# A Strassen MLP on one NeuronCore: another order of the two-level first-layer products, their sums on VectorE in quarters, residual rows added beside the fifth product, weight-sum copies issued by SyncE

## The chip, the core and the metric

The kernel runs on one core of a Trainium2 chip. Five engines with a queue each work side by side: TensorE (PE: matmul, and PEld for the weight loads), VectorE (DVE), ScalarE (ACT), GpSimd (POOL) and SyncE (SP, which here only issues DMAs). The metric is the device time of one execution in microseconds, as the median of several runs; less is better. The profile is of one further execution.

## The reference

Everything is fp32. A linear attention with a decay per head is followed by a Fourier mixing, a layer norm and an MLP; what the change touches is the MLP.

```python
x = attention(q, k, v, lam)                    # (4, 8, 768, 64) -> (4, 768, 512)
u = x + np.real(np.fft.fft(np.fft.fft(x, axis=1), axis=2))
un = (u - mean(u)) / np.sqrt(var(u) + 1e-06)   # over the 512 columns
ch = np.maximum(un @ w_ch1, 0.0) @ w_ch2       # w_ch1 (512, 2048), w_ch2 (2048, 512)
return u + ch                                  # (4, 768, 512)
```

## The kernel before

The 3072 rows go through the MLP as twelve groups of 256 rows. Four groups (PLAIN) pass a plain MLP (`mlp`, lines 636 and 650) while attention and mixing still run. The other eight (LATE) are taken as four pairs of groups, j = 0 to 3, after about 430 us, and this is the part that the change touches. Of a pair, the two layers of the MLP are computed as 2x2 block products by a Strassen scheme (Winograd's form): seven products of sums of blocks instead of eight products of blocks. `PRODUCTS` names the seven: a is a sum of weight blocks (first layer) or of hidden blocks (second layer), b the other operand.

The first layer of pairs 0 and 1 (`first_layer`, matmuls on L882) has one level. The second layer of all pairs (`deep_second`, L1023) and the first layer of pairs 2 and 3 (`deep_first`, L964) have two levels: each of the seven products is itself made of seven partial products (`seven`). A partial product is eight weight loads and eight matmul records of 128x128, into one of three PSUM banks X, Y, Z of the product: X takes partial products 0, 2, 4 and 6, Y takes 1, Z takes 3 and 5, and each must have been read before the next is put on it. The read (`read`, L971/L973 in the first layer, L1029/L1031 in the second) adds the bank to a quarter of a hidden tile; the first value of a fresh tile is copied by ScalarE instead, four of a product's seven.

The hidden tiles of a pair are `a11`, `a12`, `a22`, `s1` (also called T) and `s3` (a21). In `deep_first` products 0 to 6 come in order and are gathered into these: after product 1, T is added to a11 (L986, GpSimd) and a11 gets its relu; after product 3, a12 = T + a22 (L989, GpSimd); after product 4, a21 += T on GpSimd (L991), a22 += a21 on VectorE (L992), relu of a22, the loads of the residual rows (`load_x`), the splits (`split`, L847: one quarter becomes the difference of two) and the preparation of the second layer's first operand (`prepare_a`, L861 to L865). The helper `part_sum` does a sum in two halves of 128x1024, all on its line L939.

The sums of the second operands (`inputs`, L796 to L815 on VectorE, then nine 128x128 sums on GpSimd, L820 to L822) are made before the pair's first layer. The second-level sums of the weights are made once on GpSimd during the first layers of pairs 0 and 1 (`keep_sums`, `keep_sums_w`), put to HBM, and loaded as tiles `tx` product by product (L760, SyncE; six buffers, so two products). One of the four weight sums of a product is copied into the place of a quarter of the weights by `place_sums_w` (L745, seven DMAs issued by ScalarE).

In `deep_second` the outputs are gathered into y11, y12, y21, y22 and a tile T (`P.t`): after product 3, y21 = T + y22 (L1054, VectorE) and the residual rows are added on GpSimd (`add_u`, L1037); after product 4, y12 += T and y22 += y12 (L1057, L1058, VectorE), the residual of y22 on GpSimd (L1037) and that of y12 on VectorE (L1060, rows read backwards). Then rows are stored, one half by an indirect DMA of GpSimd (L625), the other by SyncE (L623).

The order is set by `in_step`: product k begins at step 7k and takes every second step, so that two products alternate on TensorE; the preparations of product k + 1 go between. The tile framework's scheduler then orders each engine's queue and sets semaphores; a queue is worked off in order.

```python
X, Y, Z = (bank() for _ in range(3))
for m, ps, start, where in ((0, X, True, (0, 0, 1)), (1, Y, True, (0, 0, 0)), (2, X, False, (1, 0, 1)), ...
    mm(m, ps, start)
    read(ps, *where)
    yield 0.0
```

Of the kernel before, what the change touches and what calls it, by code (L numbers as in the profile page):

```python
# [76 lines left out]
def kernel(  # L77
# [10 lines left out]
    nc = tc.nc  # L88
# [639 lines left out]
    def quarters_w(t):  # L728

        return [t[:, k, f:f + FH // 2] for f in (0, FH // 2) for k in range(2)]  # L730
# [11 lines left out]
    def place_sums_w():  # L742

        for k, (a, _) in enumerate(PRODUCTS):
            nc.scalar.dma_start(quarters_w(s2.A[a])[2], s2.sd[k][3])  # L745

# [26 lines left out]
    def inputs(j):  # L773
# [40 lines left out]
        yield 0.0  # L814
        V.tensor_tensor(t4, b21, t2, op=SUB)  # L815
        yield 0.0
        q2, q1, q4 = [new(s2.hp, [128, 3, 128], "sv", bufs=3) for _ in range(3)]
        for i, n in enumerate(("t2", "t1", "t4")):
            C11, C12, C21, C22 = (U[n][:, k, m:m + 128] for k in range(2) for m in (0, 128))
            nc.gpsimd.tensor_tensor(q2[:, i], C12, C11, op=ADD)  # L820
            nc.gpsimd.tensor_tensor(q1[:, i], C22, q2[:, i], op=SUB)
            nc.gpsimd.tensor_tensor(q4[:, i], C21, q2[:, i], op=SUB)  # L822
            P.T[n] = [q1[:, i], q2[:, i], q4[:, i]]
            yield 0.0
# [115 lines left out]

    def seven(mm, read, first=()):

        X, Y, Z = (bank() for _ in range(3))
        for m, ps, start, where in ((0, X, True, (0, 0, 1)), (1, Y, True, (0, 0, 0)), (2, X, False, (1, 0, 1)),
                                    (3, Z, True, (1, 1, 1)), (4, X, False, (1, 1, 0)), (5, Z, False, (1, 0, 0)),
                                    (6, X, False, (0, 1, 1))):
            mm(m, ps, start)
            read(ps, *where)
            yield 0.0

    def deep_first(j, k):

        P = pairs[j]
        h, (a, b) = P.h, PRODUCTS[k]
        y, fresh = (("s1", 1), ("a11", 1), ("a22", 1), ("s1", 0), ("s3", 1), ("a12", 0), ("s3", 0))[k]
        A11, A12, A3, A22 = quarters_w(s2.A[a])
        B11, T3, B21, B22 = (P.U[b][:, kt, m:m + 128] for kt in range(2) for m in (0, 128))
        (S1, S2, S4), (T1, T2, T4) = P.pre_w.pop(k), P.T[b]
        ab = [(A11, B11), (A12, B21), (S2, T2), (A3, T3), (S1, T1), (A22, T4), (S4, B22)]
# [7 lines left out]
        def read(ps, r, s, first):  # L967
# [6 lines left out]
            done[r, s] = done.get((r, s), 0) + 1  # L974
            if k > 4 and done[r, s] == (1 if (r, s) == (0, 1) else 2):
                nc.scalar.activation(o, o, AF.Relu)

        yield from seven(mm, read)

        def relu(t):  # L980
            for s in range(G):
                nc.scalar.activation(t[:, s], t[:, s], AF.Relu)

        T, a11, a12, a21, a22 = (h[n] for n in ("s1", "a11", "a12", "s3", "a22"))
        if k == 1:
            part_sum(nc.gpsimd, a11, a11, T, ADD)  # L986
            relu(a11)
        elif k == 3:
            part_sum(nc.gpsimd, a12, T, a22, ADD)  # L989
        elif k == 4:  # L990
            part_sum(nc.gpsimd, a21, a21, T, ADD)  # L991
            part_sum(V, a22, a22, a21, ADD)  # L992
            relu(a22)
            load_x(j)
            open_y(j)
            split(a11)
            run(prepare_a(j, 0))
        elif k == 5:
            split(a22)
            split(a12)  # L1000
        elif k == 6:
            split(a21)
            part_sum(V, T, a21, a22, ADD)
            if j + 1 < PAIRS:
                load_u(j + 1)

    def deep_second(j, k):
# [26 lines left out]

        def add_u(k, m, y):
            u = P.us[k][:, :, 0:HM] if m == 0 else P.us[k][:, :, DM - 1:HM - 1:-1]
            nc.gpsimd.tensor_tensor(y, y, u, op=ADD)  # L1037

        who, yt = P.who, P.yt
        if k == 0:  # L1040
            h["s2"] = h["a11"]
            if j < DEEP:
                split(h["s1"])
            part_sum(V, h["a11"], h["s1"], h["a11"], SUB)
        elif k == 1:
            V.tensor_tensor(y11, y11, T, op=ADD)  # L1046
            add_u(0, 0, y11)
        elif k == 2:
# [4 lines left out]
        elif k == 3:  # L1053
            V.tensor_tensor(y21, T, y22, op=ADD)  # L1054
            add_u(1, 0, y21)
        elif k == 4:
            V.tensor_tensor(y12, y12, T, op=ADD)  # L1057
            V.tensor_tensor(y22, y22, y12, op=ADD)  # L1058
            add_u(1, 1, y22)
            V.tensor_tensor(y12, y12, P.us[0][:, :, DM - 1:HM - 1:-1], op=ADD)  # L1060
        elif k == 5:
# [26 lines left out]
    def deep_pair(j):  # L1088

        def before(k):  # L1090
            if k == 0:
                return both(prepare_w(j, 0), inputs(j))
            return prepare_w(j, k)

# [13 lines left out]
    def in_step(work):  # L1108
# [3 lines left out]
        for at in range(7 * n + 8):  # L1112
# [5 lines left out]
            for q in sorted(live, key=abs):  # L1118
                if q < 0 or (at - 7 * q) % 2 == 0:
                    if next(live[q], live) is live:  # L1120
                        del live[q]

    def late():
        for j in range(PAIRS):
            if j < DEEP:
# [4 lines left out]
                if j + 1 < DEEP:  # L1130
                    in_step(second_layer(j) + [(inputs(j + 1), iter(()))])
        place_sums_w()
        in_step(second_layer(DEEP - 1) + [w for j in range(DEEP, PAIRS) for w in deep_pair(j)])
# [115 lines left out]
```

## Time and profile before

| | |
|---|---|
| time, median of 3 runs | 817.17 us (815.62 to 818.04) |
| the profiled execution's own time | 810.14 us |
| its span | 808.4 us |
| granted TensorE clock | 0.997 of full speed |
| busy: TensorE, VectorE, ScalarE, GpSimd | 95%, 72%, 27%, 27% of the span |
| chain that ended last, by engine | TensorE 71%, VectorE 13%, DMA 7%, issue 4% |

By stretch, the part that the change touches (us busy; the columns are the stretch, TensorE, VectorE, ScalarE, GpSimd):

| stretch | what runs | PE | DVE | ACT | POOL |
|---|---|---|---|---|---|
| 430 to 475 | pair 0, first layer | 44.8 | 42.7 | 10.9 | 38.5 |
| 475 to 520 | pair 0, second | 44.6 | 35.3 | 5.0 | 5.1 |
| 520 to 560 | pair 1, first | 40.0 | 32.9 | 9.4 | 35.3 |
| 560 to 613 | pair 1, second | 51.0 | 42.2 | 6.9 | 8.6 |
| 613 to 667 | pair 2, first (two levels) | 51.0 | 33.3 | 17.4 | 19.6 |
| 667 to 711 | pair 2, second | 43.5 | 37.9 | 5.5 | 8.2 |
| 711 to 760 | pair 3, first (two levels) | 46.0 | 30.7 | 16.7 | 16.4 |
| 760 to 801 | pair 3, second | 40.5 | 31.9 | 4.8 | 5.2 |

A line of the profile names the source line, the engine, the operation, the output and input tiles without their numbers, and the shape; in a timeline the first two columns are the start from the span's beginning and the duration in us, and in brackets stands how long the engine stood idle before it and what ended that. In a table of waits an entry reads "who waited <- for whom", with the total in us, how often, and the longest. A matmul in fp32 shows as two weight loads and two matmul records.

### The profile page before, as it was taken

What the parts mean: (1) busy time and instruction counts of PE and PEld (TensorE: products, weight loads), DVE (VectorE), ACT (ScalarE), POOL (GpSimd) and SP (SyncE); (2) the same over time, 40 slices, a digit from 0 to 9 for tenths busy, and PEclk for the clock granted to TensorE, in tenths of its full rate; (3) what the DMA queues carried; (4) which work ended last, traced back from release to release, by engine and by line L of the source; (5) the groups of instructions that cost most, each with busy time, mean ns of one, the idle gap of its engine ahead of it and who ended that gap; (6) DMA issues with size and microseconds to landing.
All of it is one profiled execution on the core that took longest, in us unless ns stands there. A gap on an engine that the chain in (4) does not pass through costs nothing.

```text
span 808.4 us, 14556 instructions
## 1 busy us (share of the span) xinstructions
PE 770.1 (95%) x5616; PEld 642.5 (79%) x5616; DVE 580.9 (72%) x1126; ACT 215.5 (27%) x504; POOL 216.3 (27%) x202
## 2 busy tenths in 40 slices
PE   6889899999999999999999999999999989999896
PEld 5777666768585857767747899988899989999896
DVE  6899898775744571345897997689866489836983
ACT  3655444225420210312101221022101331032400
POOL 3233340011020110220106930298013330235011
PEclk9999999999999999999999999999999999999998
DMA  9979624248831137440333384256845446455442
GB/s 239 249 156 256 194 81 132 66 104 208 213 100 58 53 70 152 118 162 28 65 69 125 133 272 125 76 206 230 291 125 166 136 149 191 132 162 162 125 118 79
DMA packets 152331, 116.80 MB, mean 144 GB/s; under 512 B 113998, under 2 KB 113998, under 8 KB 152262
## 3 DMA queue, kind: packets, MB, share of 16 engines
q1 hardware_dynamic: 146112, 101.56, 45.3%
q10 hardware_dynamic: 4038, 7.61, 2.6%
q0 software_dynamic: 2112, 6.69, 2.5%
q8 instruction: 45, 0.74, 0.4%
q14 instruction: 24, 0.20, 0.1%
HBM read 83.58 MB, written 32.25 MB: 143 GB/s over the span
## 4 chain that ended last, share of the span: by engine, by line
PE 71%; DVE 13%; DMA 7%; issue 4%; ACT 2%; POOL 2%; POOLq 0%; ACTq 0%; SPq 0%; DVEq 0%
PE p L1023 19%; PE p L882 12%; PE p L964 9%; PE pm L650 8%; PE pm L636 8%; DMA raw<-in_moe_w_ch_dram 3%; PE pa L516 3%; PE pa L332 3%; PE pa L298 3%; DMA x<-xb,ix 2%; PE pa L328 2%; DVE ha L939 1%; PE pa L274 1%; PE pa L315 1%; PE pa L279 1%
## 5 line engine op out<-in xcount | busy, mean ns | idle before, releaser
L636 PE MATMUL pm<-ut,w 128*128 128x256 f32 x512 | 119.2, 382 | 0.0
L650 PE MATMUL pm<-w,hr 128*128 128x512 f32 x256 | 115.8, 597 | 0.1
L636 PEld LDWEIGHTS pm<-ut,w 128*128 128x128 f32 x512 | 94.4, 190 | 15.4 <-issue 3.6
L650 PEld LDWEIGHTS pm<-w,hr 128*128 128x128 f32 x256 | 46.6, 190 | 49.5 <-issue 48.0
L1037 POOL TENSOR_TENSOR y<-y,u 128x512 f32<-128x512 f32 x12 | 16.6, 1382 | 159.4 <-DVE y L1046 105.8
L1023 PE MATMUL p<-tx,sx 128*128 128x128 f32 x416 | 55.3, 276 | 1.3 <-DVE y L1031 1.3
L1023 PEld LDWEIGHTS p<-tx,sx 128*128 128x128 f32 x416 | 50.6, 192 | 1.9 <-DVE y L1031 1.9
L270 POOL TENSOR_TENSOR kd<-k,decay 128x512 f32<-128x512 f32 x20 | 23.0, 1151 | 95.6 <-PE pa L315 40.5
L882 PE MATMUL p<-ur,w 128*128 128x256 f32 x192 | 46.9, 379 | 0.1
L882 PEld LDWEIGHTS p<-ur,w 128*128 128x128 f32 x192 | 36.3, 190 | 5.7 <-issue 0.5
L973 DVE TENSOR_TENSOR hs<-p,hs 128x512 f32<-128x512 f32 x40 | 27.4, 689 | 18.6 <-PE p L964 17.9
L1029 ACT COPY y<-p 128x128 f32<-128x128 f32 x48 | 12.8, 266 | 103.4 <-PE p L1023 102.7
L1031 DVE TENSOR_TENSOR y<-p,y 128x128 f32<-128x128 f32 x92 | 25.5, 287 | 18.8 <-PE p L1023 12.6
L1023 PE MATMUL p<-w,ha 128*128 128x128 f32 x288 | 37.7, 275 | 0.0
L302 DVE TENSOR_TENSOR sc<-pa,decay 128x512 f32<-128x512 f32 x48 | 31.5, 684 | 8.4 <-PE pa L298 8.2
L298 PEld LDWEIGHTS pa<-qT,kT 64*128 64x128 f32 x384 | 26.0, 193 | 13.2 <-ACT qT L281 7.3
L550 POOL TENSOR_SCALAR ve<-mv 128x2 f32<-128x2 f32 x12 | 3.4, 285 | 123.0 <-DVE mv L547 123.0
L1023 PEld LDWEIGHTS p<-w,ha 128*128 128x128 f32 x288 | 35.2, 192 | 0.2
L332 PE MATMUL pa<-sc,v 128*64 128x128 f32 x384 | 31.7, 281 | 3.8 <-DVE sc L302 3.7
L882 PE MATMUL p<-sx,w1s 128*128 128x256 f32 x128 | 33.1, 381 | 1.8 <-ACT ha L904 1.6
L644 ACT ACTIVATE hr<-pm 128x256 f32<-128x256 f32 x44 | 16.7, 385 | 67.4 <-PE pm L636 67.0
L298 PE MATMUL pa<-qT,kT 64*128 64x128 f32 x384 | 30.7, 292 | 3.2 <-ACT qT L281 2.9
(227 smaller groups left out, 1718.7 us busy)
## 6 DMA issues: line engine op xcount, KB each, us to landing
tx<-td SPq DMA_DIRECT2D x84, 256.0 KB, 3.0
raw<-in_moe_w_ch_dram SPq DMA_DIRECT2D x32, 512.0 KB, 5.4
tx<-sd SPq DMA_DIRECT2D x42, 256.0 KB, 2.7
sd<-tx SPq DMA_DIRECT2D x28, 256.0 KB, 2.0
k<-in_k_dram SPq DMA_DIRECT2D x24, 256.0 KB, 5.2
q<-in_q_dram SPq DMA_DIRECT2D x24, 256.0 KB, 6.1
v<-in_v_dram SPq DMA_DIRECT2D x24, 256.0 KB, 4.6
td<-tx SPq DMA_DIRECT2D x21, 256.0 KB, 2.0
```

The source lines that it names most:

```text
L270: nc.gpsimd.tensor_tensor(kd, kt, kpow, op=ALU.mult)
L298: mm(pss[hi][:, hp, :], lhsT=kT[HD[hi], hp, :], rhs=qT[HD[hi], hp, :], start=True, stop=True)
L302: nc.vector.tensor_tensor(t, pss[hi], decay[:, hi::2, :], op=ALU.mult)
L332: mm(po[HD[hi], hp, :], lhsT=vt[:, 2 * hp + hi, :], rhs=sc[hi][:, hp, :], start=(c == 0 and hp == 0), stop=(hp == HP - 1), skip_group_chec ...
L516: mm = nc.tensor.matmul(ps[0:m, n, :], lhsT=piece(a, i, n), rhs=cs[0:rows, a, i in (2, 3), n, :], start=(a == 0), stop=(a == 1))
L636: nc.tensor.matmul(ps, lhsT=w1[:, c, 128 * fc:128 * fc + 128], rhs=ut[:, c, :], start=(c == 0), stop=(c == KO - 1))
L650: nc.tensor.matmul(ps, lhsT=hr[(fc - f0) // 4][:, fc % 4, 128 * i:128 * i + 128], rhs=w2[:, fc, :], start=(fc == f0), stop=(fc == f1 - 1))
L882: nc.tensor.matmul(ps, lhsT=s2.A[a][:, kt, 128 * i:128 * i + 128], rhs=U[b][:, kt, :], start=(first and kt == 0), stop=(kt == 1), skip_gro ...
L964: nc.tensor.matmul(ps[:, 128 * i:128 * i + 128], lhsT=ab[m][0][:, 128 * i:128 * i + 128], rhs=ab[m][1], start=(start and i == 0), stop=Tru ...
L973: V.tensor_tensor(o, p, o, op=ADD)
L1023: nc.tensor.matmul(ps[:, 0:HM // 2], lhsT=ab[m][0][i], rhs=ab[m][1][:, i, :], start=(start and i == 0), stop=(i == HF // 2 - 1), skip_grou ...
L1031: V.tensor_tensor(o, ps[:, 0:HM // 2], o, op=ADD)
```

## The change

- `deep_first` takes its seven products in the order `FIRST` = 0, 3, 4, 2, 1, 5, 6. The sums between them become `quarter_sum`: VectorE, four quarters of 128x512 each, one per step, with the relu of a22 by quarters on ScalarE. a11 is no longer a fresh tile plus T; product 1 is added to it last, and its relu comes with the reads. `part_sum` on GpSimd and `relu` leave the first layer. `load_x` comes after the third product taken, the splits are spread over steps.
- `seven` yields before a partial product instead of after it, and `in_step` lets a product that is past its last partial product go on at every step.
- In `inputs` of pairs 2 and 3 the difference t4 moves from VectorE to GpSimd, after the sums of t2 and t1.
- In `deep_second`, after product 3, y22 += T on VectorE, then three adds of residual rows on GpSimd: y21 = y22 + u, T += u, y22 += u. After product 4, y22 += y12 and y12 += T. The add on VectorE (L1060) is gone.
- `place_sums_w` issues its DMAs on SyncE and is called after product 0 of the second layer of pair 1.

```diff
@@ -742,7 +742,7 @@
     def place_sums_w():
 
         for k, (a, _) in enumerate(PRODUCTS):
-            nc.scalar.dma_start(quarters_w(s2.A[a])[2], s2.sd[k][3])
+            nc.sync.dma_start(quarters_w(s2.A[a])[2], s2.sd[k][3])
 
     def load_u(j, queue=nc.sync):
 
@@ -812,11 +812,12 @@
         t2, t4 = U["t2"], U["t4"] = [sx([128, 2, G * 128]) for _ in range(2)]
         V.tensor_tensor(t2, b22, t1, op=SUB)
         yield 0.0
-        V.tensor_tensor(t4, b21, t2, op=SUB)
-        yield 0.0
         q2, q1, q4 = [new(s2.hp, [128, 3, 128], "sv", bufs=3) for _ in range(3)]
         for i, n in enumerate(("t2", "t1", "t4")):
             C11, C12, C21, C22 = (U[n][:, k, m:m + 128] for k in range(2) for m in (0, 128))
+            if n == "t4":
+                nc.gpsimd.tensor_tensor(t4, b21, t2, op=SUB)
+                yield 0.0
             nc.gpsimd.tensor_tensor(q2[:, i], C12, C11, op=ADD)
             nc.gpsimd.tensor_tensor(q1[:, i], C22, q2[:, i], op=SUB)
             nc.gpsimd.tensor_tensor(q4[:, i], C21, q2[:, i], op=SUB)
@@ -938,24 +939,27 @@
         for s in range(G):
             e.tensor_tensor(o[:, s], x[:, s], y[:, s], op=op)
 
-    def seven(mm, read, first=()):
+    def seven(mm, read):
 
         X, Y, Z = (bank() for _ in range(3))
         for m, ps, start, where in ((0, X, True, (0, 0, 1)), (1, Y, True, (0, 0, 0)), (2, X, False, (1, 0, 1)),
                                     (3, Z, True, (1, 1, 1)), (4, X, False, (1, 1, 0)), (5, Z, False, (1, 0, 0)),
                                     (6, X, False, (0, 1, 1))):
+            if m:
+                yield 0.0
             mm(m, ps, start)
             read(ps, *where)
-            yield 0.0
+
+    FIRST = [0, 3, 4, 2, 1, 5, 6]
 
     def deep_first(j, k):
 
         P = pairs[j]
-        h, (a, b) = P.h, PRODUCTS[k]
-        y, fresh = (("s1", 1), ("a11", 1), ("a22", 1), ("s1", 0), ("s3", 1), ("a12", 0), ("s3", 0))[k]
+        h, (a, b) = P.h, PRODUCTS[FIRST[k]]
+        y, fresh = (("a11", 1), ("s1", 1), ("s3", 1), ("a22", 1), ("a11", 0), ("a12", 0), ("s3", 0))[k]
         A11, A12, A3, A22 = quarters_w(s2.A[a])
         B11, T3, B21, B22 = (P.U[b][:, kt, m:m + 128] for kt in range(2) for m in (0, 128))
-        (S1, S2, S4), (T1, T2, T4) = P.pre_w.pop(k), P.T[b]
+        (S1, S2, S4), (T1, T2, T4) = P.pre_w.pop(FIRST[k]), P.T[b]
         ab = [(A11, B11), (A12, B21), (S2, T2), (A3, T3), (S1, T1), (A22, T4), (S4, B22)]
         done = {}
 
@@ -972,37 +976,48 @@
             else:
                 V.tensor_tensor(o, p, o, op=ADD)
             done[r, s] = done.get((r, s), 0) + 1
-            if k > 4 and done[r, s] == (1 if (r, s) == (0, 1) else 2):
+            if k > 3 and done[r, s] == (1 if (r, s) == (0, 1) else 2):
                 nc.scalar.activation(o, o, AF.Relu)
 
         yield from seven(mm, read)
 
-        def relu(t):
-            for s in range(G):
-                nc.scalar.activation(t[:, s], t[:, s], AF.Relu)
-
         T, a11, a12, a21, a22 = (h[n] for n in ("s1", "a11", "a12", "s3", "a22"))
+
+        def quarter_sum(o, x, y, relu=False):
+            for (s, i) in ((0, 0), (0, HF // 2), (1, HF // 2), (1, 0)):
+                o_, x_, y_ = (t[:, s, i:i + HF // 2] for t in (o, x, y))
+                yield 0.0
+                V.tensor_tensor(o_, x_, y_, op=ADD)
+                if relu:
+                    nc.scalar.activation(o_, o_, AF.Relu)
+
         if k == 1:
-            part_sum(nc.gpsimd, a11, a11, T, ADD)
-            relu(a11)
+            yield from quarter_sum(T, T, a11)
+        elif k == 2:
+            yield from quarter_sum(a21, a21, T)
+            load_x(j)
         elif k == 3:
-            part_sum(nc.gpsimd, a12, T, a22, ADD)
+            yield from quarter_sum(a12, T, a22)
+            yield from quarter_sum(a22, a22, a21, True)
+            yield 0.0
+            split(a22)
         elif k == 4:
-            part_sum(nc.gpsimd, a21, a21, T, ADD)
-            part_sum(V, a22, a22, a21, ADD)
-            relu(a22)
-            load_x(j)
             open_y(j)
+            yield 0.0
             split(a11)
-            run(prepare_a(j, 0))
+            yield 0.0
+            yield from prepare_a(j, 0)
         elif k == 5:
-            split(a22)
+            yield 0.0
             split(a12)
         elif k == 6:
-            split(a21)
-            part_sum(V, T, a21, a22, ADD)
             if j + 1 < PAIRS:
                 load_u(j + 1)
+            yield 0.0
+            split(a21)
+            for s in range(G):
+                yield 0.0
+                V.tensor_tensor(T[:, s], a21[:, s], a22[:, s], op=ADD)
 
     def deep_second(j, k):
 
@@ -1032,9 +1047,9 @@
 
         yield from seven(mm, read)
 
-        def add_u(k, m, y):
+        def add_u(o, y, k, m):
             u = P.us[k][:, :, 0:HM] if m == 0 else P.us[k][:, :, DM - 1:HM - 1:-1]
-            nc.gpsimd.tensor_tensor(y, y, u, op=ADD)
+            nc.gpsimd.tensor_tensor(o, y, u, op=ADD)
 
         who, yt = P.who, P.yt
         if k == 0:
@@ -1042,22 +1057,24 @@
             if j < DEEP:
                 split(h["s1"])
             part_sum(V, h["a11"], h["s1"], h["a11"], SUB)
+            if j == DEEP - 1:
+                place_sums_w()
         elif k == 1:
             V.tensor_tensor(y11, y11, T, op=ADD)
-            add_u(0, 0, y11)
+            add_u(y11, y11, 0, 0)
         elif k == 2:
             if j < DEEP:
                 split(h["a22"])
             h["s4"] = h["a12"]
             part_sum(V, h["a12"], h["a12"], h["s2"], SUB)
         elif k == 3:
-            V.tensor_tensor(y21, T, y22, op=ADD)
-            add_u(1, 0, y21)
+            V.tensor_tensor(y22, y22, T, op=ADD)
+            add_u(y21, y22, 1, 0)
+            add_u(T, T, 0, 1)
+            add_u(y22, y22, 1, 1)
         elif k == 4:
+            V.tensor_tensor(y22, y22, y12, op=ADD)
             V.tensor_tensor(y12, y12, T, op=ADD)
-            V.tensor_tensor(y22, y22, y12, op=ADD)
-            add_u(1, 1, y22)
-            V.tensor_tensor(y12, y12, P.us[0][:, :, DM - 1:HM - 1:-1], op=ADD)
         elif k == 5:
             store(*who[1][1], yt[:, 1, 1])
         else:
@@ -1089,8 +1106,8 @@
 
         def before(k):
             if k == 0:
-                return both(prepare_w(j, 0), inputs(j))
-            return prepare_w(j, k)
+                return both(prepare_w(j, FIRST[0]), inputs(j))
+            return prepare_w(j, FIRST[k])
 
         def begin():
             open_pair(j)
@@ -1116,7 +1133,7 @@
                 if k + 1 < n:
                     live[-k - 1] = iter(work[k + 1][0])
             for q in sorted(live, key=abs):
-                if q < 0 or (at - 7 * q) % 2 == 0:
+                if q < 0 or (at - 7 * q) % 2 == 0 or at - 7 * q > 12:
                     if next(live[q], live) is live:
                         del live[q]
 
@@ -1129,7 +1146,6 @@
                 first_layer(j)
                 if j + 1 < DEEP:
                     in_step(second_layer(j) + [(inputs(j + 1), iter(()))])
-        place_sums_w()
         in_step(second_layer(DEEP - 1) + [w for j in range(DEEP, PAIRS) for w in deep_pair(j)])
 
 
```

## The prediction

> **What bounds the kernel now.** I read first the page (busy shares, forty slices), then TensorE's waits where the diff's functions run, then the timeline at each. TensorE is busy 95% of the 808.4 us span at a granted clock of 0.997, and holds 71% of the chain of waits. The change leaves the matmuls as they are, so it can win only time in which TensorE stands still. As compiled, both kernels are the same up to the first L882 matmul (430 us).
>
> TensorE's waits from 440 us on; columns: total us, times, longest:
>
> ```profile
> PE p L964 <- DVE ha L973: 3.9, 2, 1.9
> PE p L964 <- DVE hs L973: 2.2, 2, 1.1
> PE p L882 <- ACT ha L904: 1.6, 1, 1.6
> PE p L1023 <- DVE y L1031: 1.3, 3, 0.5
> ```
>
> These are all, and they are of three kinds, which the timeline shows (start, duration, instruction). In the two-level layers a partial product is eight weight loads (PEld); one follows the other every 0.893 us (nine from 601.50 to 609.54). I call this a slot; what exceeds it is lost.
>
> Kind A, at 516, 611 and 703 us: the residual's row on VectorE.
>
> ```profile
> 608.96 1.75 DVE L1060 TENSOR_TENSOR y<-y,u 128x512 f32<-128x512 f32 x1
> 609.54 0.97 PEld L1023 LDWEIGHTS p<-tx,ha 128*128 128x128 f32 x8
> ...
> 611.16 0.97 PEld L1023 LDWEIGHTS p<-tx,sx 128*128 128x128 f32 x8 [0.65 <-DVE y L1031]
> ```
>
> The read (L1031) that frees the bank stands behind L1060 and comes at 610.63. Lost: 1.62 - 0.89 = 0.73; at 703 us 0.73 again, at 516 us 0.67.
>
> Kind B, at 653 and 745 us: sums between products, on GpSimd and VectorE.
>
> ```profile
> 652.31 3.35 DVE L939 TENSOR_TENSOR ha<-ha,hs 128x1024 f32<-128x1024 f32 x1 [1.57 <-POOL hs L939]
> ...
> 653.31 0.97 PEld L964 LDWEIGHTS p<-ur,w1s 128*128 128x128 f32 x8
> ...
> 655.59 0.68 DVE L973 TENSOR_TENSOR ha<-p,ha 128x512 f32<-128x512 f32 x1
> ...
> 656.38 0.97 PEld L964 LDWEIGHTS p<-sv,w 128*128 128x128 f32 x8 [2.10 <-issue]
> ...
> 657.92 0.68 DVE L973 TENSOR_TENSOR hs<-p,hs 128x512 f32<-128x512 f32 x1
> ...
> 658.66 0.97 PEld L964 LDWEIGHTS p<-sx,tx 128*128 128x128 f32 x8 [1.31 <-DVE hs L973]
> ```
>
> The reads L973 wait in VectorE's queue behind an L939 sum. Lost: 3.07 - 0.89 = 2.18 and 2.28 - 0.89 = 1.39, together 3.57; the same at 745 us.
>
> Kind C, once: the weight-sum copies on ScalarE.
>
> ```profile
> 564.76 0.84 PEld L882 LDWEIGHTS p<-sx,w 128*128 128x128 f32 x4
> ...
> 567.18 0.37 ACT L904 COPY ha<-p 128x256 f32<-128x256 f32 x1 [4.22 <-DMA tx<-td]
> ...
> 567.60 0.73 PEld L882 LDWEIGHTS p<-sx,w1s 128*128 128x128 f32 x4 [2.00 <-ACT ha L904]
> ```
>
> The weight loads of the product that L904 copies ended at 563.03 (four of the eight from 562.17), but the first DMA of L745 stands ahead of it on ScalarE and waits for a tile load to land. Lost: 2.84 - 0.86 (four loads of this form) = 1.98, and 0.22 at 569.44, where a later copy follows a later L745.
>
> **What the Trainium skill says.** "SBUF — State Buffer", section "Who interferes with whom": a VectorE instruction with two SBUF inputs and a GpSimd instruction that reads SBUF exclude each other, and the later one blocks entirely. The trace agrees: L939 took 3.35 us beside a GpSimd sum and 1.21 alone, L1060 1.75 beside a GpSimd add and 0.69 alone (792.57). Reads with one PSUM input keep their 0.69 beside a GpSimd sum (644.69). "VectorE: DVE Perf Modes", section on the TRN2 errata, prices an fp32 tensor_tensor at (N+151)/0.96 ns, 691 ns for 512 elements; the trace has 684 to 692. Back to back, though, they start every 0.60 us (659.12, 659.72, 660.32), and that pitch I use. "PSUM — Partial Sum Buffer", section on bank collisions, asks that a bank be guarded by semaphores, so a late read holds the next product back: TensorE went on at 658.66, 0.06 after the read's end at 658.60.
>
> **The change, part by part.**
>
> 1. *Another order of the first layer's products, sums in quarters* (pairs 2 and 3). Gone per pair: six GpSimd sums of 128x1024 (2.36 us each), two VectorE sums (3.35 and 1.21), four L982 activations (1.06 each). New: twenty VectorE sums of 128x512 at a pitch of 0.60, 12.0 us, and eight activations of 0.63, on a ScalarE that was busy 17.4 of the 54 us from 613 to 667. VectorE was busy 33.3 of these 54 us, so the sum fits, but only if it is spread. I therefore laid the changed kernel's compiled VectorE order beside the slots by hand. Product k begins at slot 7k and uses every second slot. A read can start 1.20 us after its slot's first weight load (797.58 to 798.78), and its bank is wanted four slots, 3.57 us, after that load: a read may be 3.57 - 1.20 - 0.68 = 1.69 us late. Up to slot 40 no more than one quarter stands between two reads, and none is over 0.4 us late. From the read of slot 28 to that of slot 54 there are 38 instructions of 0.60 and one of 0.20, 23.0 us, in 26 slots and one read, 23.8 us. Within it the two splits and three preparations for the second layer, at slots 41 to 43, make a heap: the read of slot 46 is 1.53 late, 0.1 us short of a stall. Later reads catch up. At the second layer's entry (three kinds of 1024-wide sums, 1.21 each, there before as well) one read is 0.15 us too late. So kind B goes, 2 x 3.57 = 7.14, and 2 x 0.15 = 0.3 comes. Bounds: no new loss at all, 7.1 won; or a pitch of 0.69 (the duration) throughout, 38 x 0.09 = 3.4 more, less 0.8 spare and 0.1 slack, 2.5 per pair, which leaves 2.1. That a sum itself comes late for TensorE I exclude: no product reads one before slot 49.
>
> 2. *Residual rows beside the fifth product* (all pairs). L1060 leaves VectorE (1.75 us three times, 0.69 in the last pair, where nothing waited), so kind A goes: 2.13 us. GpSimd does three adds in a row after the fourth product instead of one and later another; by L1037 1.26 + 1.58 + 1.58 = 4.4 us, from 601.6 to about 606.1. VectorE's sum y22+y12 now waits for them, with reads queued behind it; a sum with the same inputs started at 606.88 (L1057), so 0.8 us are to spare, in the last pair 0.4. But L863 and L865, two SBUF inputs each, now meet an add and can block for up to 1.6 us, and the reads behind them with them. Those had 0.3 to 0.6 us of idle ahead of them and 2.1 us of slack (1.69 + 0.68 - 0.28). I take 0.1 us lost in three pairs, 0.3 in all. Bounds: none; or one whole add of 1.58 over the slack in every pair, 6.3.
>
> 3. *Copies by SyncE.* L745 leaves ScalarE, kind C goes: 2.20 us. On SyncE the seven copies stand, as compiled, behind the six tile loads of 564 us and six of them ahead of the load of the next pair's inputs (L751), which at 572.58 waited for the last L882 products, as these copies must. Behind them are tiles that are wanted some 10 us later. At 0.4 us per issue the seven cost SyncE 2.8 us that nothing waits for: 0. If a tile were late it would cost up to a landing, 2.9 us (median of tx<-td).
>
> 4. *t4 on GpSimd.* VectorE loses 0.69 and a wait of 1.49 for TensorE (L815, 619.50) in each deep pair; no product stood still there. GpSimd waits instead, with only t4's own sums behind it; they are wanted at slot 35, some 25 us later. 0.
>
> 5. *Order of yields, earlier residual loads.* The loads now wait for GpSimd's adds of the pair before, long done; 0.
>
> Sum: -7.14 - 2.13 - 2.20 = -11.47, + 0.3 + 0.3 = -10.9. The profiled execution took 810.14 us (span 808.4, so 1.7 around it): 797.5 and 799.2 after. The median of the runs shown is 7.0 above that execution, a difference that I carry over: 817.17 - 10.9 = 806.3.
>
> **Rivals.**
>
> *Half of it comes back (smaller gain).* VectorE is 95% full from slot 28 to 54, so kind B returns in small pieces, 2.5 us a pair by the pitch of 0.69, and GpSimd's three adds cost 1 us in each of three pairs: -11.5 + 5.0 + 3.0 = -3.5, 813.7 us. For it: the read of slot 46 has 0.1 us left. Against: pitches of 0.60 for a dozen in a row from 658.52 to 663.91.
>
> *No measurable gain.* The gaps go, but others as large come: tiles late on SyncE twice (5.8) beside the former loss of 4.4: -1.3, 815.9. Against: the list of waits has none on a tile, and the tiles run two products ahead.
>
> *VectorE becomes the bound (slower).* Place: slots 28 to 54 of pairs 2 and 3. If each of the 38 took not 0.60 but 0.69 plus 0.20 us of waiting for a semaphore (the idle that stands before many reads), 38 x 0.29 = 11.0, less 0.9 spare: 10.1 a pair, +20.2 - 11.5 = +8.7, 825.9 us. It decides from 0.60 + (5.7 + 0.9)/38 = 0.77 us on. Against: those 0.20 occur where VectorE was ahead of TensorE, not in a backlog.
>
> **How the numbers follow.** The forecast (803.5 to 809) has 0.64; the smaller gain (809 to 814.7) 0.20; no gain 0.07; slower 0.09. A measurement of this kernel tells from no change about 0.3%, 2.5 us. Faster by more: 0.64 + 0.20 = 0.84; within: 0.07; slower: 0.09. The range goes from 803.5 (all of 11.5 won, 1 us of other small slips, 1.2 us of the median's spread) to 813.0, which takes in most of the smaller gain; a fifth is left out.
>
> **What would show it.** Right: no TensorE wait for the reads of the two first layers, weight loads every 0.893 us through slots 28 to 60; none behind the y22+y12 sum; the L904 copy within 0.5 us of its product; no GpSimd sums in the first layers and VectorE over 40 us busy per first layer. Wrong: new waits of TensorE on VectorE at slots 46 to 50 or at the second layer's entry, or on tiles; VectorE sums of 128x512 that take over 1 us; a granted clock below 0.99.

## The result, and the profile after

| | before | after |
|---|---|---|
| time, median (range) | 816.72 us (815.26 to 818.04, 6 runs) | 803.52 us (800.95 to 807.19, 6 runs) |
| ratio to before, 95% interval | | 0.9841 [0.9811, 0.9871] |
| the profiled execution's own time | 810.14 us | 800.95 us |
| its span, granted clock | 808.4 us, 0.997 | 799.0 us, 0.998 |

The kernel became 1.6% faster. In a later session the changed kernel took 802.85 us (801.16 to 805.85), ratio 0.984 [0.9769, 0.991].

The page of the kernel after; the second row and those like it give busy time, share of the span and number of instructions:

```profile
span 799.0 us, 14578 instructions
...
PE 768.3 (96%) x5616; PEld 642.5 (80%) x5616; DVE 587.6 (74%) x1148; ACT 217.4 (27%) x512; POOL 195.0 (24%) x196
```

Line numbers are those of each run's own kernel. In after, the read of the first layer is L977 (L973 before), that of the second L1046 (L1031), and ScalarE's copy L905 (L904).

TensorE is as busy as before to 0.2% (768.3 against 770.1 us) in a span that is 9.4 us shorter: what went is standstill. VectorE took over a part of what GpSimd gave up. All TensorE waits from 425 us on (total, times, longest) are now two; the second, of 0.2 us, is there before as well:

```profile
PE p L1038 <- DVE t L1046: 1.4, 1, 1.4
PE p L883 <- DVE sx L786: 0.2, 1, 0.2
```

I also added up, over all weight loads after 475 us, the time by which each group started later than the group before it lasts. Before it is 12.71 us, after it 2.26. The part of the span before 429 us, the same instructions in both, took 0.75 us longer this time. -10.45 + 0.75 = -9.7, to be compared with the spans' -9.4.

**Kind A** is gone. The timeline of after at the place where 0.73 us was lost (start, duration):

```profile
603.24 1.34 DVE L864 TENSOR_TENSOR sx<-sx,ha 128x512 f32<-128x512 f32 x1
...
603.99 1.72 POOL L1052 TENSOR_TENSOR y<-y,u 128x512 f32<-128x512 f32 x1
...
605.27 0.98 DVE L866 TENSOR_TENSOR sx<-ha,sx 128x512 f32<-128x512 f32 x1 [0.29 <-PE p L1038]
...
606.98 0.68 DVE L1076 TENSOR_TENSOR y<-y 128x512 f32<-128x512 f32 x1
...
608.54 0.97 PEld L1038 LDWEIGHTS p<-w,ha 128*128 128x128 f32 x8
609.43 0.97 PEld L1038 LDWEIGHTS p<-tx,ha 128*128 128x128 f32 x8
610.32 0.97 PEld L1038 LDWEIGHTS p<-tx,sx 128*128 128x128 f32 x8
```

The weight loads keep their 0.89 us. GpSimd's last add ends at 605.71, 1.27 us before L1076, the sum that needs it. Two VectorE sums were held up beside these adds, in each of the four pairs alike: L864 took 1.34 us and L866 0.98 instead of 0.68. Nothing of the 0.96 us that they lost per pair reached TensorE.

**Kind B** is gone. The timeline of after where 3.57 us were lost in each pair:

```profile
651.44 1.28 DVE L848 TENSOR_TENSOR ha<-ha 128x512 f32<-128x512 f32 x2
...
652.31 0.97 PEld L968 LDWEIGHTS p<-ur,w1s 128*128 128x128 f32 x8
...
652.64 0.69 DVE L977 TENSOR_TENSOR hs<-p,hs 128x512 f32<-128x512 f32 x1
653.20 0.97 PEld L968 LDWEIGHTS p<-sv,w 128*128 128x128 f32 x8
653.24 0.68 DVE L862 TENSOR_TENSOR y<-ha 128x512 f32<-128x512 f32 x1
653.84 0.69 DVE L977 TENSOR_TENSOR ha<-p,ha 128x512 f32<-128x512 f32 x1
654.10 1.87 PEld L968 LDWEIGHTS p<-sx,tx 128*128 128x128 f32 x16
```

VectorE starts something every 0.60 us without a pause, and the reads (L977) stand between the splits and preparations (L848, L862), so that no read is far behind its bank. From 613 to 667 us VectorE was busy 41.98 us (33.25 before), from 711 to 760 us 42.86 (30.71).

**Kind C** is gone: L905, the copy that waited for L745, now waits 0.49 us for TensorE and for nothing else. But the copies have brought the one wait that is left:

```profile
570.28 1.10 SPq L745 DMA_DIRECT2D w1s<-sd  x2
...
571.78 0.93 SPq L751 DMA_DIRECT2D ur<-utd  x2
...
574.86 1.22 DVE L940 TENSOR_TENSOR ha<-hs,ha 128x1024 f32<-128x1024 f32 x1
...
577.35 0.97 PEld L1038 LDWEIGHTS p<-tx,sx 128*128 128x128 f32 x8
...
579.01 0.69 DVE L796 TENSOR_TENSOR ur<-ur 128x512 f32<-128x512 f32 x1 [2.93 <-DMA ur<-utd]
579.62 0.28 DVE L1046 TENSOR_TENSOR t<-p,t 128x128 f32<-128x128 f32 x1
...
579.96 0.97 PEld L1038 LDWEIGHTS p<-w,sx 128*128 128x128 f32 x8 [1.63 <-DVE t L1046]
```

L751 loads the inputs of pair 2. SyncE issues it after six copies (L745). VectorE's first sum of these inputs, L796, comes up at 576.08 and stands until the load has landed at 579.0; the read L1046 is queued behind it, and TensorE's next product waits for the read. Lost: 2.61 - 0.89 = 1.72 us; in the later profile of the same kernel 2.61.

Two things had to meet. Counted from the weight loads of the product `tx,sx` at 571.99 (573.81 before), the load is issued at -0.21 (-1.23 before) and lands up to 6.5 us after its issue (5.9 before); and L796 has a place in VectorE's queue at +4.09, where it stood at +7.97 before (581.78). With the old place the late load would just have been in time (+7.02).

### The profile page after: what moved, and what is told of

The parts are those of the page before. It is cut to its first block, busy times and chain, and to the rows that moved or that the text cites. A ratio compares the mean times of both kernels' runs of the same rounds, so it can differ in the third digit from the quotient of the medians.

```text
span 799.0 us, 14578 instructions
## 1 busy us (share of the span) xinstructions
PE 768.3 (96%) x5616; PEld 642.5 (80%) x5616; DVE 587.6 (74%) x1148; ACT 217.4 (27%) x512; POOL 195.0 (24%) x196
## 4 chain that ended last, share of the span: by engine, by line
PE 77%; DVE 11%; DMA 5%; issue 4%; ACT 1%; POOL 1%; POOLq 0%; ACTq 0%; SPq 0%; DVEq 0%
PE p L1038 20%; PE p L883 12%; PE p L968 11%; PE pm L650 10%; PE pm L636 8%; PE pa L332 3%; PE pa L516 3%; PE pa L298 3%; DMA x<-xb,ix 2%; PE pa L328 2%; DMA w<-sd 1%; PE pa L274 1%; PE pa L315 1%; DVE sc L302 1%; PE pa L348 1%
## 5 line engine op out<-in xcount | busy, mean ns | idle before, releaser
L1052 POOL TENSOR_TENSOR y<-y,u 128x512 f32<-128x512 f32 x12 | 18.8, 1568 | 200.8 <-DVE y L1063 159.0
L1046 DVE TENSOR_TENSOR y<-p,y 128x128 f32<-128x128 f32 x92 | 25.4, 287 | 22.2 <-PE p L1038 15.8
L332 PEld LDWEIGHTS pa<-sc,v 128*64 128x64 f32 x384 | 23.6, 140 | 11.3 <-DVE sc L302 5.5
```

Of the source, the lines that this page charges most:

```text
L332: mm(po[HD[hi], hp, :], lhsT=vt[:, 2 * hp + hi, :], rhs=sc[hi][:, hp, :], start=(c == 0 and hp == 0), stop=(hp == HP - 1), skip_group_chec ...
L1046: V.tensor_tensor(o, ps[:, 0:HM // 2], o, op=ADD)
L1052: nc.gpsimd.tensor_tensor(o, y, u, op=ADD)
```

## The experiments

Every ratio is to the kernel before, run in the same sessions. "Slips" are the sums of lost TensorE time as above.

### Undoing the parts, one at a time

*u_first*: the first layers of pairs 2 and 3 as before (order of products, sums on GpSimd in halves, yields), the rest changed.

```diff
-    FIRST = [0, 3, 4, 2, 1, 5, 6]
+    FIRST = list(range(7))
...
         if k == 1:
-            yield from quarter_sum(T, T, a11)
-        elif k == 2:
-            yield from quarter_sum(a21, a21, T)
-            load_x(j)
+            part_sum(nc.gpsimd, a11, a11, T, ADD)
+            relu(a11)
```

> The first layers of pairs 2 and 3 (order of products, sums, yields) as before; residual rows, copies and t4 as changed. Theory (three separate stalls, each ended by one part): the 3.57 us per pair of TensorE behind VectorE's half sums return, so the span is 799.0 + 7.1 = 806.1 and the time about 7 us above the changed kernel. Rival (the gain of this part came from elsewhere, or VectorE has room and takes the sums in any order): less than 3 us above the changed kernel.

Measured: 814.27 us (808.79 to 821.01, 20 runs), ratio 0.9978 [0.9953, 1.0002], span 810.9. The two stalls of kind B are back in each pair, 2.19 and 1.38 us, 7.14 in all. So this part, order, sums and yields together, carries nearly the whole gain. The span is 11.9 us above that of after, more than 7.14: behind each stall TensorE runs slowly for a while. The timeline of the weight loads, eight of which take 0.97 us at full clock:

```profile
652.50 0.97 PEld L967 LDWEIGHTS p<-ur,w1s 128*128 128x128 f32 x8
655.58 1.43 PEld L967 LDWEIGHTS p<-sv,w 128*128 128x128 f32 x8 [2.10 <-issue]
657.85 1.78 PEld L967 LDWEIGHTS p<-sx,tx 128*128 128x128 f32 x8 [0.85 <-DVE hs L976]
```

The windows of the same kernel (columns: stretch, its length, then busy time and instruction count of PE, PEld, DVE, ACT and POOL, then the granted clock, DMA share, GB/s):

```profile
652.00:656.00 4.00, 2.06 (x18) 1.90 (x18) 4.00 (x3) 1.06 (x1) 1.78 (x1) 1.00 0.95 327
656.00:660.00 4.00, 3.45 (x17) 3.15 (x16) 4.00 (x7) 1.69 (x2) 0.00 (x0) 0.50 0.14 54
660.00:664.00 4.00, 4.00 (x26) 4.00 (x26) 3.50 (x7) 1.17 (x2) 0.00 (x0) 0.65 0.48 116
```

After TensorE was busy for only 2.06 of 4 us, its clock is half for nearly 7 us. The slips in the slow stretches behind the stalls add up to 3.9 us in the two pairs (0.77, 0.21, 0.81, 0.57; 0.77, 0.21, 0.55).

*u_residual*: the residual rows as before, the last add (here on L1077) on VectorE.

```diff
         elif k == 3:
-            V.tensor_tensor(y22, y22, T, op=ADD)
-            add_u(y21, y22, 1, 0)
-            add_u(T, T, 0, 1)
-            add_u(y22, y22, 1, 1)
+            V.tensor_tensor(y21, T, y22, op=ADD)
+            add_u(1, 0, y21)
         elif k == 4:
-            V.tensor_tensor(y22, y22, y12, op=ADD)
             V.tensor_tensor(y12, y12, T, op=ADD)
+            V.tensor_tensor(y22, y22, y12, op=ADD)
+            add_u(1, 1, y22)
+            V.tensor_tensor(y12, y12, P.us[0][:, :, DM - 1:HM - 1:-1], op=ADD)
```

> The residual rows added as before (one add on VectorE, two on GpSimd), all else as changed. Theory: three stalls of 0.7 us return at the end of the second layers of pairs 0 to 2, span 799.0 + 2.1 = 801.1. Rival (the three adds in a row on GpSimd cost VectorE as much as the one add they replace): within 0.7 us of 799.0.

Measured: 804.55 us (802.41 to 806.83, 4 runs), ratio 0.9844 [0.9798, 0.9891], span 803.2. Slips of 0.66, 0.73 and 0.73 us are back, 2.12 in sum, at the three places of kind A:

```profile
611.33 1.75 DVE L1077 TENSOR_TENSOR y<-y,u 128x512 f32<-128x512 f32 x1
```

The medians can't tell this gain from none (0.9844 and 0.9841); the timeline can. The other 2.1 us of the span come from the stall at 577 us, 0.75 longer this time, and half clock behind it (1.63).

*u_copies*: the copies on ScalarE, called before the layer, as before.

```diff
-            nc.sync.dma_start(quarters_w(s2.A[a])[2], s2.sd[k][3])
+            nc.scalar.dma_start(quarters_w(s2.A[a])[2], s2.sd[k][3])
...
-            if j == DEEP - 1:
-                place_sums_w()
...
+        place_sums_w()
         in_step(second_layer(DEEP - 1) + ...
```

> The seven weight-sum copies issued by ScalarE and called before the layer, as before; all else as changed. Theory: ScalarE's copy waits behind the first of them again and TensorE loses 2.2 us at 565; the new stall of 1.7 us at 577 us in the changed kernel, put down to these copies standing ahead of the load of pair 2's inputs on SyncE, goes: span 799.0 + 2.2 - 1.7 = 799.5. Rival (the stall at 577 us has nothing to do with the copies' place; the VectorE order puts the first sum of those inputs too early): both stalls stand, span 801.2.

Measured: 804.02 us (803.71 to 806.11, 4 runs), ratio 0.9847 [0.9805, 0.9889], span 802.1 (3 us of which come from a slower start, before 35 us). Kind C is back, 2.52 and 0.70 us of slips, and the stall at 577 us is gone: L796 stands at +7.98 behind its reference product here, the old place. In the timeline ScalarE waits for a tile load with L905 behind the copy:

```profile
570.37 0.33 ACTq L745 DMA_DIRECT2D w<-sd  x1
570.74 0.37 ACT L905 COPY ha<-p 128x256 f32<-128x256 f32 x1 [4.76 <-DMA tx<-td]
...
571.16 0.73 PEld L883 LDWEIGHTS p<-sx,w1s 128*128 128x128 f32 x4 [2.55 <-ACT ha L905]
```

Moving the copies to SyncE took away 3.2 us here and gave back 1.7 to 2.6 at 577 us: 0.6 to 1.5 us are left in the timelines, and nothing that the medians show (0.9847 and 0.9841).

### The copies without the new stall

*copies_pin1*: copies still on SyncE, held in program order after product 1 of the layer, so that the load of the inputs is issued ahead of them.

```diff
-            nc.sync.dma_start(quarters_w(s2.A[a])[2], s2.sd[k][3])
+            tc.keep_in_program_order(nc.sync.dma_start(quarters_w(s2.A[a])[2], s2.sd[k][3]))
...
-            if j == DEEP - 1:
-                place_sums_w()
         elif k == 1:
             V.tensor_tensor(y11, y11, T, op=ADD)
             add_u(y11, y11, 0, 0)
+            if j == DEEP - 1:
+                place_sums_w()
```

> The copies on SyncE, but in program order after product 1 of pair 1's second layer, so that the inputs' load (L751) stands ahead of them. Theory: the load lands some 2 us sooner, the stall at 577 us falls from 1.7 to below 0.5, span 797.3 to 797.8. Rival (order of VectorE alone makes the stall): 1.2 us or more of it stay, span 798.5 or more.

Measured: 801.22 us (799.35 to 802.66, 4 runs), ratio 0.9798 [0.9757, 0.984], span 800.7, in which the part before 432 us took 4 us longer than in after, with half-clock stretches at 28 and 72 us. After 480 us no slip over 0.17 us. Run again beside the next kernels:

> The same kernel as copies_pin1, in the same rounds as old_pin1. Theory: about 801 us, 1.5 to 2.5 us below the changed kernel (its one stall of 1.72 to 2.61 us at 577 us is gone), no slip over 0.3 us after 475 us, clock 0.995 to 0.998. Rival (the stall only moves: tiles come late behind the copies instead): a new stall of 1 us or more on a tile between 570 and 600 us, and a time within 0.5 us of the changed kernel.

Measured: 799.45 us (798.17 to 802.27, 6 runs), ratio 0.9789 [0.9753, 0.9824], span 796.4. The timeline:

```profile
569.86 0.80 SPq L751 DMA_DIRECT2D ur<-utd  x2
...
575.77 0.69 DVE L796 TENSOR_TENSOR ur<-ur 128x512 f32<-128x512 f32 x1
```

L796 keeps its early place (it starts at +4.24), and no wait is shown ahead of it; the load is issued at -1.67. No tile came late. So the load behind the copies made the stall at 577 us.

### Which half of the new first layer did it

*order_gpsimd*: the new order of products, but sums of 128x1024 on GpSimd: eight per pair, where the kernel before has six there and two on VectorE.

```diff
-            for (s, i) in ((0, 0), (0, HF // 2), (1, HF // 2), (1, 0)):
-                o_, x_, y_ = (t[:, s, i:i + HF // 2] for t in (o, x, y))
+            for s in range(G):
                 yield 0.0
-                V.tensor_tensor(o_, x_, y_, op=ADD)
+                nc.gpsimd.tensor_tensor(o[:, s], x[:, s], y[:, s], op=ADD)
```

> The new order of the products, but the sums between them whole (halves of 128x1024) on GpSimd instead of in quarters on VectorE; all else as changed. Theory (order and quarters are needed together): after the fourth product GpSimd has four sums of 2.36 us in a row, 9.4 us, and the split of a22 waits for them in VectorE's queue with reads behind it, so 3 to 6 us a pair are lost in the first layers, span 805 to 811. Rival (the order alone ended the stall): under 1 us a pair, span below 801.

Measured: 813.38 us (809.17 to 817.72, 20 runs), ratio 0.9965 [0.9945, 0.9985], span 810.7. One stall per pair, 3.88 and 3.86 us, with half clock behind both. The timeline at the first:

```profile
649.99 2.34 POOL L989 TENSOR_TENSOR ha<-ha,hs 128x1024 f32<-128x1024 f32 x1
...
652.37 1.06 ACT L991 ACTIVATE ha<-ha 128x1024 f32<-128x1024 f32 x1 [3.68 <-POOL ha L989]
...
653.46 0.69 DVE L848 TENSOR_TENSOR ha<-ha 128x512 f32<-128x512 f32 x1 [5.37 <-ACT ha L991]
654.06 2.48 DVE L977 TENSOR_TENSOR ha<-p,ha 128x512 f32<-128x512 f32 x4
```

GpSimd works off its sums at 2.35 us each, the relu follows the last, the split L848 waits for the relu with VectorE idle for 5.37 us, and four reads wait behind it. With the sums on GpSimd the new order of products gains almost nothing.

*quarters_oldorder*: the old order of products, all sums on VectorE in quarters.

```diff
-    FIRST = [0, 3, 4, 2, 1, 5, 6]
+    FIRST = list(range(7))
...
-            yield from quarter_sum(T, T, a11)
+            yield from quarter_sum(a11, a11, T, True)
...
         elif k == 4:
+            load_x(j)
+            run(quarter_sum(a21, a21, T))
+            run(quarter_sum(a22, a22, a21, True))
+            split(a22)
```

> The sums in quarters on VectorE, but the products in the order of before (so a21 and a22 can only be summed after the fifth product, eight quarters at once before the last product's reads); all else as changed. Theory: a heap of five to eight sums of 0.60 us stands before the reads of slots 41 and 42, 3.0 to 4.8 us against 1.7 of slack: 1.3 to 3.1 us a pair lost, span 801.6 to 805.2. Rival (quarters alone ended the stall): under 0.7 us a pair, span below 800.4.

Measured: 801.91 us (800.26 to 803.5, 4 runs), ratio 0.9823 [0.9755, 0.9891], span 798.9. No stall in the first layers; the only one is that of 577 us (1.71). The theory that order and quarters are needed together fell. I had expected the eight sums that come in a row after product 4 to hold up the reads; in the timeline five of them end just in time:

```profile
649.71 0.68 DVE L990 TENSOR_TENSOR hs<-hs,hs 128x512 f32<-128x512 f32 x1
650.30 0.68 DVE L990 TENSOR_TENSOR ha<-ha,hs 128x512 f32<-128x512 f32 x1
650.91 0.68 DVE L990 TENSOR_TENSOR hs<-hs,hs 128x512 f32<-128x512 f32 x1
651.51 1.28 DVE L990 TENSOR_TENSOR ha<-ha,hs 128x512 f32<-128x512 f32 x2
652.71 0.68 DVE L977 TENSOR_TENSOR ha<-p,ha 128x512 f32<-128x512 f32 x1
```

*halves_oldorder*: as the last, but the sums in halves of 128x1024, as the kernel before cuts them. It separates the engine from the size.

```diff
-        def quarter_sum(o, x, y, relu=False):
-            for (s, i) in ((0, 0), (0, HF // 2), (1, HF // 2), (1, 0)):
-                o_, x_, y_ = (t[:, s, i:i + HF // 2] for t in (o, x, y))
+        def half_sum(o, x, y, relu=False):
+            for s in range(G):
                 yield 0.0
-                V.tensor_tensor(o_, x_, y_, op=ADD)
+                V.tensor_tensor(o[:, s], x[:, s], y[:, s], op=ADD)
```

> The old order of the products with every sum between them on VectorE, as in quarters_oldorder, but cut as the kernel before cuts it: halves of 128x1024 (1.21 us when nothing excludes them) instead of quarters of 128x512. It separates the engine from the size. Theory (what made kind B is GpSimd's queue and the exclusion: an L939 of 3.35 us with the reads behind it): no stall over 0.5 us at 653 and 745 us, TensorE's slips in each first layer below 1 us together, span 798 to 801, the 577 us stall of 1.7 to 2.7 us still there. Rival (the small size is needed: four halves in a row after product 4 are 4 x 1.21 = 4.8 us, more than the reads' slack of 1.69 us): one stall per pair of 1.5 to 3 us near 650 and 742 us, span 802 to 806, ratio about 0.988.

Measured: 803.2 us (799.28 to 808.49, 4 runs), ratio 0.9812 [0.9764, 0.986]. Its profile fell on the longest of the four, span 806.7, because of half-clock stretches at 24 to 36, 296 to 304 and 584 to 592 us; of the two first layers it shows a slip of 0.06 us in each. Three halves in a row, and the read behind them:

```profile
658.63 1.21 DVE L989 TENSOR_TENSOR hs<-hs,hs 128x1024 f32<-128x1024 f32 x1
659.76 2.35 DVE L989 TENSOR_TENSOR ha<-ha,hs 128x1024 f32<-128x1024 f32 x2
662.03 0.68 DVE L977 TENSOR_TENSOR ha<-p,ha 128x512 f32<-128x512 f32 x1
```

Neither the order nor the quarters are needed. What ended kind B is that the sums left GpSimd. One thing is left open: the new yields are in all the kernels without kind B, and in order_gpsimd, where they did not end the stalls; whether sums on VectorE would be enough without them no run shows.

*old_pin1*: quarters_oldorder with the copies of copies_pin1.

> quarters_oldorder together with the copies of copies_pin1 (on SyncE, held behind product 1 of the second layer of pair 1 and behind the residual load): the old order of the products, quarters on VectorE. Theory (the order of products contributes nothing; the 577 us stall is the residual load queued behind the copies): no TensorE slip over 0.3 us after 475 us, span 797 to 799, time about 801, equal to copies_pin1 within 0.3%. Rival (the new order is worth something once the 577 us stall is gone): at least 1 us of slips in the two first layers and a time 1 us or more above copies_pin1_again in the same rounds.

Measured: 799.04 us (798.48 to 801.82, 6 runs), ratio 0.9782 [0.9747, 0.9818], span 798.0, no slip over 0.17 us after 475 us. It equals copies_pin1 in the same rounds (799.45), without the new order. By medians both are some 0.5% faster than the changed kernel; but the intervals of the ratios overlap a little (they end at 0.9818 and 0.9824, that of the changed kernel begins at 0.9811), so from the times alone this is likely and not certain. That the stall of 1.7 to 2.6 us is gone is seen in all three profiles.

### How much room VectorE has

*dose2*: behind each quarter sum a second VectorE instruction of its size, max of the quarter with itself, which leaves the values as they are.

```diff
                 V.tensor_tensor(o_, x_, y_, op=ADD)
+                V.tensor_tensor(o_, o_, o_, op=ALU.max)
```

> The changed kernel with a second VectorE instruction of the same size (a maximum of the quarter with itself) behind each of the twenty quarter sums of a first layer. Theory (VectorE is 95% full from slot 28 to 54 and nearly idle before): the six sums there add 3.6 us a pair to 0.9 us of room, so about 2.7 us a pair are lost at slots 40 to 50, span 799.0 + 5.4 = 804.4. Rival (VectorE has room left, the bound is far): under 1 us a pair. Second rival (VectorE was the bound already): all 12 us a pair show, span above 815.

Measured: 809.06 us (805.29 to 810.6, 12 runs), ratio 0.9895 [0.9863, 0.9926], span 806.0. New slips per pair: 0.99 + 0.31 + 0.63 in the first layer and 0.38 + 0.44 behind it in the second, 2.75 us. TensorE's waits in the two first layers are on the reads again:

```profile
PE p L968 <- DVE ha L977: 1.5, 2, 0.7
```

So VectorE can become the bound. Of the 16 instructions per pair, nine stand behind the read of slot 28 (641 us): 5.4 us at the pitch of 0.60, of which 2.75 reached TensorE. The rest went into the spare room and the reads' slack.

*after_again* is the changed kernel once more, beside order_gpsimd, quarters_oldorder and dose2; its numbers stand with the result.

> The changed kernel once more, beside these. If the time saved beyond the stalls' length (13.2 us measured against 10.4 by the stalls of the two profiles) comes from a higher granted clock, its runs show a mean clock about 0.004 above that of the kernel before; if it is chance of the runs, the clocks are alike and the ratio is nearer to 0.987.

## Why the prediction was right, point by point

The forecast was 806.3 us, the time 803.52: inside the range from 803.5 to 813.0, by 0.02 us, with faster as the likeliest sign. That it lies just inside is luck; the 802.85 of the later session would not. The chain of reasons held in the main. Two terms were off, in opposite directions: the profiled execution gained 1.7 us less than forecast (points 3 and 5), and the median came 4.4 us nearer to the profiled execution (point 6). The second was the larger, which is why the kernel was faster than the forecast.

1. *Kind B, -7.14*: held. u_first brings back 7.14 us of slips, to the digit. The allowance of 0.3 at the second layer's entry didn't come: no slip over 0.1 us there. The spare room was judged rightly by the pitch of 0.60 us (pitches of 0.60 from 652.64 to 653.84 above); the "smaller gain" with 0.69 is out. The count of 38 instructions and a short one between the reads of slots 28 and 54 is right, too; the twenty quarter sums, 12.0 us, are really sixteen, 9.6 us. The account of the remedy was too broad, though: I treated order, quarters and engine as one. quarters_oldorder, halves_oldorder and old_pin1 show that the change of engine is enough, at least with the new yields. On GpSimd the sums held VectorE up in two ways: before, it stood 1.57 us until GpSimd's first half was ready, and its own sum then took 2.14 us longer than alone (3.35 against 1.21). The runs don't price the two apart; in order_gpsimd it was the waiting (5.37 us). The second is the mutual exclusion that the Trainium skill tells of ("SBUF — State Buffer", section "Who interferes with whom"): the L939 half that took 3.35 us beside GpSimd takes 1.21 in halves_oldorder, with no GpSimd sum about.

2. *Kind A, -2.13, and +0.3 for GpSimd's adds*: the first held (2.12 came back in u_residual). The second was an upper guess: the blocking happened (1.34 and 0.98 against 0.68 us) and the slack took it.

3. *Kind C, -2.20, copies on SyncE 0*: here a step failed. "At 0.4 us per issue the seven cost SyncE 2.8 us that nothing waits for: 0" was wrong by 1.72 us. I had named the load L751 as standing behind the copies, and then asked only when the tiles are wanted, not when VectorE wants what L751 loads. I looked neither at the new place of L796 in VectorE's queue, 3.9 us earlier, nor at who stands behind it. The bound given for a late transfer, 2.9 us, does cover it: it was 1.7 to 2.6.

4. *t4 on GpSimd, order of yields: 0*. Nothing in the trace of after speaks against it: no TensorE wait names these lines. Neither was tried alone.

5. *The sum against its own execution*: -10.9 forecast, -9.2 measured (810.14 to 800.95). The stalls give -11.47 + 1.72 - 0.7 (small slips of 0.1 to 0.18 us that are gone too) = -10.45, and 0.75 was lost in the part that both have in common.

6. *The median*: "The median of the runs shown is 7.0 above that execution, a difference that I carry over" failed in the kernel's favour. After, the median is only 2.6 above the profiled execution. Most of the 7.0 belongs to the granted clock: the profiled execution of before had 0.997, while 65 further runs of it had medians of 0.990 and 0.991 (0.984 to 0.997). A difference of 0.006 to 0.007 in 810 us is 5 us. The runs of after had a median of 0.9955 and 0.996. The change removed the stalls behind which the clock falls, and with them, it seems, some 4 us (0.005 x 810) that no wait in the profile of before showed. That this is why the clock rose is a reading with good support, not a proof: the kernels with kind B or its like (before, u_first, order_gpsimd) have median clocks of 0.990 to 0.991, all others 0.9955 to 0.9975.

Of the rivals, "no gain" was right in its mechanism (a transfer late behind the copies) and wrong in its size and number: one stall, not two of 2.9 us. "VectorE becomes the bound" would have needed over 0.77 us per instruction; dose2, with 5.4 us more in the same stretch where the rival supposed 11.0, shows how it begins.

## What to carry to other kernels

When a sum on GpSimd stands beside VectorE work with two SBUF inputs, compare the engine's price with the block that it puts on the other queue: VectorE had room for all of them here, and the gain came without the new order and the smaller pieces that were also written for it. When DMA issues are moved to another queue, list every transfer that ends up behind them, and for each the first instruction that reads it and what is queued behind that one. Before a median is carried over from one kernel to another, look at the granted clock of its runs: the stalls that are to be removed may be in it twice.

## What the runs showed of the hardware that I had not expected

The granted clock falls to 0.50 after stalls shorter than expected, and not always. After stalls of 3.88 and 3.86 us (order_gpsimd) and after the pairs of 2.19 and 1.38 us in u_first it fell each time, for 3.41 or 6.83 us; after the pairs of 2.18 and 1.39 us in the profiled execution of before it stayed at 1.00. The stall at 577 us gives a series: with 2.47 (u_residual) and 2.72 us (halves_oldorder) it fell, with 2.61 (after_again), 2.73 (dose2) and 1.71 to 1.99 us (after, quarters_oldorder, u_first) it did not, nor with the 2.52 us at 568 us in u_copies. The windows of halves_oldorder:

```profile
584.00:588.00 4.00, 1.56 (x8) 1.51 (x8) 2.46 (x5) 0.27 (x1) 0.00 (x0) 0.77 0.94 357
588.00:592.00 4.00, 4.00 (x31) 4.00 (x31) 3.77 (x7) 0.80 (x3) 0.00 (x0) 0.80 0.02 8
```

The clock records of the thirteen traces show what decides. In each trace, every change of the clock comes a whole multiple of 3.413 us after the first record. Cut the traces into windows on this grid, and add up in each window the time in which TensorE neither multiplies nor loads weights (the ends of its matmuls are modelled). From 430 us on, the clock fell behind every window at full clock with 1.91 us or more of such idle time (1.91 and 2.25 in u_first, 2.15 in halves_oldorder, 2.19 in u_residual, 2.77 and 3.35 in order_gpsimd), and behind none with 1.83 or less (1.83 in dose2, 1.75 in before, 1.56 in after_again). The idle stretch of dose2 at 577 us, 2.46 us, is longer than the 2.19 of u_residual, but an edge of the grid divides it into 1.83 and 0.63. Before 430 us, where other products run, the line is lower and less sharp: the clock fell behind windows with 1.58 to 1.83 us, and others with up to 1.58 kept it. So about half of a window was enough here, and whether a stall costs clock depended on where the edge fell. This is read from the traces after the fact; no run was made to test it.

The Trainium skill, "TensorE: Matmul & The Clock Gate", Part 1, tells of a half rate after an idle window of about 3.4 us that runs freely, so that it isn't aligned with the kernel. The traces agree on the length, 3.413 us, and on the free running: the first clock record stands anywhere from 10.87 to 14.13 us after the span's start. That 1.91 us of idle time was enough does not fit a window that has to be idle from end to end; here the measurement decides. A stall of 2 to 3 us may thus cost another 1.5 to 1.6 us: behind that of 2.47 the slips were 0.46 + 0.82 + 0.35 = 1.63, behind that of 2.72 they were 1.47.
